# Loading each group's weights in three parts, behind three row tiles in a row, in a fused gated-mix forward and backward kernel

## The chip, the cores and the metric

One Trainium2 chip, one core. The time is the device time of the whole program in microseconds (us). The kernel before takes 1472.38 us (median of 3 runs, 1470.64 to 1474.87). All runs told here fell in the fast state; verdicts are faster, same or slower at 2%, with a 95% interval.

## The reference, cut to what matters

```python
def _fwd_reference(A_x, A_w_r, A_w_i, B_x, B_w_gate, B_w_up, B_w_down, gate_w):
    x = A_x                                                  # 1 x 2048 x 576, bf16
    g = _sigmoid((x * gate_w).sum(-1, keepdims=True))
    a = irfft2(rfft2(x) * (A_w_r + 1j * A_w_i))              # spectral branch
    b = (gelu(x @ B_w_gate) * (x @ B_w_up)) @ B_w_down       # F = 4608
    return g * a + (1 - g) * b
# reference: the output and the gradients of all seven differentiable inputs for one grad_out
```

## The kernel before

The hidden dimension F = 4608 is worked through in 18 groups g of 256 columns (`FG`). Each group has four row tiles m of 512 rows. In a row tile TensorE forms `z` (gradient of the hidden value, from wdT) and `xy` (gate and up, from wgu); ACT and DVE make `A`, `dHg`, `dHu` of them, which go to HBM scratch. Between these matmuls TensorE does the weight gradients of the group before and steps of the spectral branch, whose PSUM tile `pf` is taken from the pool of `z`, which has one buffer.

The loads and stores of the groups in this argument are issued by one engine, SP (`LD = nc.sync`), in program order.

```python
unit = Unit(ctx.enter_context(tc.tile_pool(name="unit", bufs=NUNIT, side="right")))   # NUNIT = 19
wpool = hstack.enter_context(tc.tile_pool(name="wpool", bufs=2, side="right"))
pz = ps1.enter_context(tc.tile_pool(name="pz", bufs=1, space=PSUM))     # z, and pf from group 1 on
# ... cut ...
def load_w(g):                       # nine DMAs
    fsl = slice(g * FG, (g + 1) * FG)
    wgu = wpool.tile([P, 5, 2 * FG], BF16, tag="wgu", name="wgu")
    wdT = wpool.tile([P, 5, FG], BF16, tag="wdT", name="wdT")
    for k, w in enumerate((B_w_gate, B_w_up)):
        cols = slice(k * FG, (k + 1) * FG)
        LD.dma_start(wgu[:, 0:4, cols], w[0:512, fsl].rearrange("(c p) f -> p c f", p=P))
        for r in (LO, HI):
            LD.dma_start(wgu[r, 4, cols], w[512:D, fsl])
    LD.dma_start_transpose(wdT[:, 4:5, :], B_w_down[fsl, DCH[4][0]:D])
    LD.dma_start_transpose(wdT[:, 0:4, :], B_w_down[fsl, 0:512])
    LD.dma_start(wdT[LO, 4, :], wdT[HI, 4, :])
    return wgu, wdT
# ... cut: one step of the inverse transform, inside s1 ...
    vps = pftile()                   # PSUM from pz
    # four matmuls into vps
    Vt = unit([2, DF], name="Vt")    # a buffer of the shared ring
    nc.scalar.copy(Vt[:], vps[:, :, :DF])
    LD.dma_start(dst[i], Vt[:])      # scr_p <- Vt
# ... cut: end of a row tile (g, m), pr = 4 g + m ...
    flush(len(stores) - 1)           # issues the waiting stores (A, dHg, dHu; o) but the last entry
    if pr == 1:
        early_loads()                # wts[1] = load_w(1), and gwb, a row of gate_w
    # ... cut ...
    if m == 0 and g >= 1 and g + 1 < NG:
        wts[g + 1] = load_w(g + 1)
```

Behind the groups a last stage of jobs reads the scratch back by transposing DMAs (`pin`), multiplies with w_down, w_gate and w_up transposed (`wd_all`, `wgT`, `wuT`) and writes two outputs.

```python
for i, (kind, t) in enumerate(jobs):
    if i > 1 and wT_loads:           # six loads: in front of jobs 2 to 7
        load_wuT(*wT_loads.pop(0))
    # ... cut ...
    else:                            # the last job
        gate_grad()                  # 80 matmuls of one column, then two stores of single numbers (out_7)
        x_last(t)
```

## Time and profile before

| | before |
|---|---|
| span of the profiled run | 1469.9 us |
| TensorE busy | 1446.1 us, 98% |
| DVE, ACT busy | 58%, 47% |
| half clock ahead of the end | 3.41 us from 285.58 us, and again from 1446.11 us |

The busy shares, the waits of TensorE, the timelines around the one wait of a row tile and the clock behind it stand in the prediction.

### The profile page before, as it was taken

Reading aid. Unit: us, or ns where it says so; the run is one execution under the profiler, and the core shown is the slowest. Engines: PE = TensorE matmul, PEld = TensorE weight load, DVE = VectorE, ACT = ScalarE, POOL = GpSimd, SP = SyncE. Lnnn points to the kernel's source line nnn. Section 1 sums busy time; section 2 is a strip of 40 time slices with the busy share of each in tenths; the row PEclk is TensorE's granted clock in tenths of the full one; section 3 lists DMA queues with packets and bytes.
Section 4 is the critical chain, followed back from the end, with each engine's and each line's share of the span. In section 5 each row is a group of like instructions: output and inputs, shape, how many; then the busy total and the mean of one; then the engine's idle time right before and its main releaser. Section 6 shows DMA issues by size and latency. Waiting matters only on the chain.

```text
span 1469.9 us, 30099 instructions
## 1 busy us (share of the span) xinstructions
PE 1446.1 (98%) x11808; PEld 1069.9 (73%) x11808; DVE 846.4 (58%) x2258; ACT 691.4 (47%) x1355; POOL 118.7 (8%) x203
## 2 busy tenths in 40 slices
PE   7999999899999999999999999999999999999998
PEld 5766667577677777677677677678877777777776
DVE  7697677788888887676776776774000541211110
ACT  5776666566766676666666666663000000000000
POOL 1000011010011001001001001000000110000000
PEclk9999999999999999999999999999999999999999
DMA  5144444444544434443534544757999997878773
GB/s 189 55 132 122 126 120 120 137 132 128 154 141 145 122 101 139 124 119 114 145 106 116 151 123 109 166 132 152 268 187 201 216 199 161 172 156 164 158 150 75
DMA packets 483963, 210.49 MB, mean 143 GB/s; under 512 B 307883, under 2 KB 473932, under 8 KB 483820
## 3 DMA queue, kind: packets, MB, share of 16 engines
q1 hardware_dynamic: 474220, 188.06, 54.1%
q0 software_dynamic: 7792, 19.49, 4.4%
q8 instruction: 92, 1.51, 0.5%
q10 hardware_dynamic: 1808, 1.02, 0.2%
q14 instruction: 51, 0.42, 0.1%
HBM read 40.89 MB, written 93.82 MB: 92 GB/s over the span
## 4 chain that ended last, share of the span: by engine, by line
PE 91%; DVE 4%; DMA 1%; ACT 1%; issue 0%; SPq 0%; DVEq 0%; ACTq 0%
PE acc L930 28%; PE wps L440 17%; PE xy L330 16%; PE wps L423 9%; PE z L318 8%; PE wps L453 2%; PE xy L325 2%; PE pf L683 2%; PE z L321 1%; PE pf L671 1%; PE pf L490 1%; DMA pin<-scr 1%; PE fx L490 0%; DVE Vt L510 0%; DVE om L383 0%
## 5 line engine op out<-in xcount | busy, mean ns | idle before, releaser
L930 PEld LDWEIGHTS <-pin 128*128 128x128 bf16 x3456 | 338.6, 98 | 89.4 <-DMA pin<-scr 3.4
L330 PE MATMUL xy<-wgu,xT 128*128 128x512 bf16 x1152 | 271.5, 380 | 0.0
L440 PEld LDWEIGHTS <-xn 128*128 128x128 bf16 x2304 | 225.3, 98 | 32.4 <-issue 0.2
L330 PEld LDWEIGHTS <-xT 128*128 128x128 bf16 x1152 | 106.9, 98 | 137.3 <-issue 30.4
L343 ACT ACTIVATE da<-z,omg 128x256 bf16<-128x256 f32 x288 | 113.4, 475 | 149.6 <-PE z L321 146.5
L947 ACT COPY bo<-acc 128x288 f32<-128x288 f32 x32 | 12.8, 399 | 311.2 <-PE acc L930 286.6
L423 PE MATMUL wps<-dB,A 128*128 128x288 bf16 x1152 | 154.2, 286 | 0.0
L318 PE MATMUL z<-wdT,dOT 128*128 128x256 bf16 x1152 | 139.2, 275 | 6.6 <-ACT Vt L634 5.1
L930 PE MATMUL acc<-wd_all,pin 128*128 128x288 bf16 x1152 | 142.9, 286 | 2.8 <-DMA pin<-scr 2.8
L930 PE MATMUL acc<-wgT,pin 128*128 128x288 bf16 x1152 | 145.3, 288 | 0.0
L930 PE MATMUL acc<-wuT,pin 128*128 128x288 bf16 x1152 | 143.6, 286 | 0.0
L423 PEld LDWEIGHTS <-A 128*128 128x128 bf16 x1152 | 112.7, 98 | 35.6
L440 PE MATMUL wps<-dHg,xn 128*128 128x256 bf16 x1152 | 134.4, 273 | 0.0
L440 PE MATMUL wps<-dHu,xn 128*128 128x256 bf16 x1152 | 131.5, 273 | 0.0
L318 PEld LDWEIGHTS <-dOT 128*128 128x128 bf16 x1152 | 111.9, 98 | 24.7 <-issue 10.9
L349 ACT ACTIVATE q<-xy 128x512 bf16<-128x512 f32 x144 | 86.0, 597 | 69.3 <-PE xy L330 65.7
L1004 DVE SCALAR_TENSOR_TENSOR f32t<-gwf,dlog,b16t 128x576 f32<-128x576 f32 x16 | 13.1, 818 | 182.7 <-DMA b16t<-dxa_scr 182.7
L356 DVE TENSOR_SCALAR s<-q 128x512 bf16<-128x512 bf16 x144 | 42.8, 297 | 100.6 <-ACT q L349 98.9
L373 ACT ACTIVATE om<-s 128x512 bf16<-128x512 bf16 x144 | 92.0, 639 | 8.3 <-DVE s L357 8.1
L374 ACT ACTIVATE s<-s 128x512 bf16<-128x512 bf16 x144 | 90.9, 631 | 4.6
L446 POOL DMA_DIRECT2D out_dram<-dw x67 | 48.8, 729 | 539.9 <-ACT dw L401 277.4
L357 DVE TENSOR_TENSOR s<-xb,s 128x512 bf16<-128x512 bf16 x144 | 61.3, 426 | 49.7 <-ACT xb L354 43.6
(182 smaller groups left out, 1807.2 us busy)
## 6 DMA issues: line engine op xcount, KB each, us to landing
scr<-A SPq DMA_DIRECT2D x144, 128.0 KB, 2.1
scr<-dHg SPq DMA_DIRECT2D x144, 128.0 KB, 2.0
scr<-dHu SPq DMA_DIRECT2D x144, 128.0 KB, 2.0
out_dram<-dw POOLq DMA_DIRECT2D x67, 128.0 KB, 2.6
wd_all<-in_B_w_down_dram SPq DMA_DIRECT2D x3, 1728.0 KB, 13.2
out_dram<-dwd POOLq DMA_DIRECT2D x34, 144.0 KB, 2.4
scr_p<-Vt SPq DMA_DIRECT2D x32, 144.5 KB, 2.2
Vp<-scr_p SPq DMA_DIRECT2D x16, 289.0 KB, 3.2
```

The costliest lines, as they stand in the source:

```text
L318: nc.tensor.matmul(zo(t), lhsT=dOT[:, ci, t, :], rhs=wdT[:, ci, :], start=(t % 4 < 2 and ci == 0), stop=False)
L330: nc.tensor.matmul(xy[k][:, t % 2, :], lhsT=xT[:, ci, t, :], rhs=wgu[:, ci, :], start=False, stop=(ci == 3))
L343: nc.scalar.activation(da[:, tt, :], z[:, tt, k, :], ACT.Copy, scale=omg32[:, t:t + 1])
L349: nc.scalar.activation(q[:], xy[:, :, 0:FG], ACT.Square)
L356: V.tensor_scalar(s[:], q[:], A_GELU, 1.0, op0=ALU.mult, op1=ALU.add)
L357: V.tensor_tensor(s[:], xb[:], s[:], op=ALU.mult)
L373: nc.scalar.activation(om[:], s[:], ACT.Sigmoid, scale=-2.0 * C_GELU)
L374: nc.scalar.activation(s[:], s[:], ACT.Sigmoid, scale=2.0 * C_GELU)
L423: nc.tensor.matmul(wps[:, :288], lhsT=tl(0, t)[:, fch * P:(fch + 1) * P], rhs=dB[:, t, h * 288:(h + 1) * 288], start=(t == 0), stop=(t == ...
L440: nc.tensor.matmul(wps[:, cc, :], lhsT=xn[:, t, (c0 + cc) * P:(c0 + cc + 1) * P], rhs=tl(k, t), start=(t == 0), stop=(t == T - 1))
L446: wst[0].dma_start(ov[:, c0:c0 + TPB, fsl], dw[:])
L930: nc.tensor.matmul(acc[:, :288], lhsT=src[:, r, :], rhs=w_of(r)[:, h * 288:(h + 1) * 288], start=(first and r == 0), stop=(last and r == F ...
```

## The change

The intent is to spread the loads: w_gate's part of the next group behind row tile 0, w_up's behind row tile 1, w_down's transposes behind row tile 2. The row of gate_w moves behind row tile 3 of group 0.

```diff
-    def load_w(g):
+    wts = {}
+
+    def load_w(g, part):
+
         fsl = slice(g * FG, (g + 1) * FG)
# ... cut: the two tiles are made in part 0 ...
+        if part < 2:
+            w, cols = (B_w_gate, B_w_up)[part], slice(part * FG, (part + 1) * FG)
             LD.dma_start(wgu[:, 0:4, cols], w[0:512, fsl].rearrange("(c p) f -> p c f", p=P))
             for r in (LO, HI):
                 LD.dma_start(wgu[r, 4, cols], w[512:D, fsl])
+        else:
+            LD.dma_start_transpose(wdT[:, 4:5, :], B_w_down[fsl, DCH[4][0]:D])
+            LD.dma_start_transpose(wdT[:, 0:4, :], B_w_down[fsl, 0:512])
+            LD.dma_start(wdT[LO, 4, :], wdT[HI, 4, :])
# ... cut: the unused load_dOT goes; the first group is loaded in three calls ...
             flush(len(stores) - 1)
-            if pr == 1:
-                early_loads()
+            if m < 3 and g + 1 < NG:
+                load_w(g + 1, m)
+            if pr == 3:
+                LD.dma_start(gwb[:], gate_w.partition_broadcast(P))
# ... cut ...
-            if m == 0 and g >= 1 and g + 1 < NG:
-                wts[g + 1] = load_w(g + 1)
```

The instructions of TensorE, ACT, DVE and GpSimd keep their order and number; only what they wait for differs. SP has the same 985 DMAs in another order.

## The prediction

> **What bounds the kernel now.** I read the busy shares first, then the waits of TensorE, then the place of the largest wait on three engines, then the granted clock around it.
>
> The first line of the page settles how much any change of loads can win:
>
> ```profile
> PE 1446.1 (98%) x11808; PEld 1069.9 (73%) x11808; DVE 846.4 (58%) x2258; ACT 691.4 (47%) x1355; POOL 118.7 (8%) x203
> PE 91%; DVE 4%; DMA 1%; ACT 1%; issue 0%; SPq 0%; DVEq 0%; ACTq 0%
> ```
>
> TensorE is busy 1446.1 of 1469.9 us, and the chain that ended last (second line) is 91% TensorE. Work on TensorE is the same in both kernels, instruction for instruction, so at most the 23.8 us of idle time, plus whatever slows it while it is busy, can change. Where the idle time lies, the list of TensorE's waits says (what waited, for what: total us, times, longest):
>
> ```profile
> PE z L318 <- ACT Vt L634: 5.1, 1, 5.1
> PE tp L283 <- DMA xn<-in_A_x_dram: 4.8, 1, 4.8
> PE acc L930 <- DMA pin<-scr: 2.8, 2, 1.5
> PE fx L490 <- DVE xT L292: 2.3, 1, 2.3
> PE z L318 <- ACT Y L496: 1.2, 2, 0.8
> ```
>
> No wait for a weight tile (wgu, wdT) is in it: the weights arrive in time, and spreading them cannot win anything by bringing them earlier. The start (xn), the head (fx) and the last stage (pin) do not touch these loads. What is left is one wait of 5.1 us, once in 18 groups. The timelines of the three engines there (start, us, what, idle before and its releaser), PE first, then ACT, then the load and store queue SP:
>
> ```profile
> 278.33 1.91 PE L440 MATMUL wps<-dHg,xn 128*128 128x256 bf16 x16
> 285.39 3.43 PE L318 MATMUL z<-wdT,dOT 128*128 128x256 bf16 x16 [5.15 <-ACT Vt L634]
> ...
> 278.89 0.38 ACT L401 CAST dwd<-wps 128x288 bf16<-128x288 f32 x1
> 284.70 0.64 ACT L634 CAST Vt<-pf 128x578 bf16<-128x578 f32 x1 [5.43 <-DMA scr_p<-Vt]
> ...
> 272.73 0.37 SPq L389 DMA_DIRECT2D scr<-dHu  x1
> 273.15 0.46 SPq L217 DMA_DIRECT2D wgu<-in_B_w_gate_dram  x1
> 273.66 1.20 SPq L219 DMA_DIRECT2D wgu<-in_B_w_gate_dram  x2
> 274.90 0.59 SPq L217 DMA_DIRECT2D wgu<-in_B_w_up_dram  x1
> 275.53 1.15 SPq L219 DMA_DIRECT2D wgu<-in_B_w_up_dram  x2
> 276.73 1.26 SPq L220 DMA_TRANSPOSE wdT<-in_B_w_down_dram  x1
> 278.03 1.29 SPq L221 DMA_TRANSPOSE wdT<-in_B_w_down_dram  x1
> 279.42 0.54 SPq L222 DMA_DIRECT2D wdT<-wdT  x1
> 280.05 0.54 SPq L609 DMA_DIRECT2D out_dram<-o  x1
> 280.69 0.44 SPq L610 DMA_DIRECT2D out_dram<-o  x1
> 281.22 4.47 SPq L635 DMA_DIRECT2D scr_p<-Vt  x3
> ```
>
> Read it from the end. TensorE wants the accumulator z at 280.24, but z shares a single buffer with the spectral tile pf, which ACT empties into a Vt tile (L634) only at 284.70, because that Vt tile still waits for an older Vt to be stored. That older Vt was written by ACT at 272.99 to 273.63; its store is issued at 281.22 and lands at 284.62 (3.40 us later in the chain of waits). The store was ready 7.6 us before it was issued: nine weight DMAs held the queue from 273.15 to 279.96, 6.8 us.
>
> One thing more, from the view by windows around the wait (stretch, length, busy time of the engines, then PEclk, DMA share, GB/s):
>
> ```profile
> 285.40:289.00 3.60, 3.60 (x20) 2.35 (x21) 1.06 (x2) 0.00 (x0) 0.71 (x1) 0.53 0.68 201
> ```
>
> The granted clock is 0.53, where every stretch around it has 1.00. That is why the 16 matmuls of z take 3.43 us here and 1.91 us in other row tiles: the wait is paid again in busy time.
>
> **What the Trainium skill says.** The page "TensorE: Matmul & The Clock Gate", in "What's actually happening", says that an idle window of some 3.4 us drops the TensorE clock to 4/8 and that a busy window of the same length restores it. The trace agrees: 5.15 us idle, then 0.53 of the clock over 3.6 us; its clock record is half speed for 3.41 us. The page "DMA: Bandwidth & Descriptors", in "Anatomy of one DMA", says that a wait for a semaphore happens on the issuing sequencer ahead of dispatch[...]. The trace agrees[...]: SP issues strictly one after the other, so whatever stands behind a waiting or long DMA is late, and the Vt stores land 2.2 us (median) after issue. The same page, in "Rules for kernel authors", advises to issue a DMA early and wait on it late; the third part of the new load is issued later than now, so this is where the change could lose.
>
> **The change part by part.** Nothing is removed or added in number: the queue has the same DMAs with the same bytes, in another order. Before, the nine DMAs of a group's weights stand together behind the first row tile m=0 (for the first group behind m=1, with gate_w's row). After, three (w_gate) stand behind m=0, three (w_up) behind m=1, and two transposes with one copy behind m=2; gate_w's row comes after m=3.
>
> Hold of the queue at one point, from the rows above: part 1 is 0.46+1.20, about 1.75 us with gaps; part 2 is 0.59+1.15, about 1.8; part 3 is 1.26+1.29+0.54 plus the copy's wait, about 3.3 to 4. So the longest hold falls from 6.8 to about 4 us.
>
> Around 273 us: part 1 ends at about 274.9. The two stores of o were ready then (DVE finished o at 273.76), and are out by about 275.6. The Vt store is issued at about 275.6 to 276 and not 281.22, and lands 3.4 us later at 279.0 to 279.4. ACT gets to its next Vt at 279.27 at the earliest (behind L401). It runs to about 280.0, and TensorE wants z at 280.24. The 5.15 us go, with perhaps 0.2 left. With the idle stretch goes the half clock: 3.41 us at half speed is 1.7 us of work. Sum: 5.15 + 1.7 = 6.85 us.
>
> **What could be given back.** I laid the new order over the old trace: each store ready when its producer ended, each DMA as long as it was, each landing as late as it was. The weights then come in time: for groups 2 to 17 the last of wdT lands 6 to 15 us ahead of the first z (a row tile takes 12 to 15 us, and the third part lags the start of its row tile by 0 to 6 us). The narrow one is group 1: in group 0 DVE lags, the third part is issued at 89.4 to 92 us, and z of group 1 starts at 95.4. With the usual 3.3 us from issue to landing (median of the wdT DMAs) it lands at 94; with the longest seen, 5.7 us, at 96.4, a loss of 1 us. I put 0.3 us. Stores behind part 2 and 3 get up to 4 us later than now; the one that a Vt then waits for is o at 309 us (landing 310.2 before, 313.7 after, while ACT wants the tile at 311.6), and TensorE needs it by 314.5, so it just fits. I put 0.3 us on such things.
>
> Total: 1472.4 - 6.85 + 0.6 = 1466.1, rounded to 1466 us, a ratio of 0.9957.
>
> **The rivals.**
> 1. *Nothing changes* (1470 to 1473). The wait would have another cause than the queue, or would move to the next full tile. Against it: the releaser named is the landing of scr_p, and its store stands right behind the weights. For it: ring slots and the eight DMA semaphores, each waited on before it is used again, could hold the Vt elsewhere.
> 2. *A new wait takes its place.* The transposes, now last, come late at each group: 17 groups times 1 us would be 1483 us or more. Against it: margins of 6 us and more, but for group 1. Or a later hold of 4 us meets another Vt store: one event would give back 2 to 7 us (1468 to 1473), as a wait over some 3.4 us costs the clock too.
> 3. *Contention eases* since 640 KB no longer come at one point. Against a gain: no wait for these transfers is on TensorE's list, and its matmuls (L330 median 379 ns, longest 390) are not stretched in the windows of the loads. Worth 0.
>
> **Range and chances.** The idle time tied to these loads is one event, so the gain is capped near 7 us, half a per cent. Runs of before spread from 1470.6 to 1474.9, which is as wide as a third of the range. I take 1462.5 to 1471. Faster by over 2% would need 29 us, more than all of TensorE's idle time: 0.01. Slower by over 2% needs a stall of 1.7 us in each group: 0.01. Within 2%: 0.98.
>
> **What would show it.** Right: TensorE's list of waits has no "z <- ACT Vt" of 5 us, its idle time is about 18.5 us, not 23.8, its busy time falls by about 1.7 us though it runs the same instructions, the mean granted clock goes from 0.998 to nearly 1, and SP issues the scr_p store within 3 us of the Vt. Wrong: a line where z or xy waits for DMA wdT or wgu; a stretch with the clock near 0.5 elsewhere; a wait of ACT for out_dram<-o or scr_p over 3 us near the end of a row tile; or the old wait still there with another releaser.

## More of the kernel before

In the last stage TensorE waits twice for a `pin` tile (timeline of TensorE: start, us, what, idle time before it and its releaser):

```profile
1106.83 8.99 PE L930 MATMUL acc<-wd_all,pin 128*128 128x288 bf16 x72 [1.36 <-DMA pin<-scr]
1117.27 4.95 PE L930 MATMUL acc<-wd_all,pin 128*128 128x288 bf16 x39 [1.45 <-DMA pin<-scr]
```

And in the last microseconds (the list of DMA issues: what, engine, count, KB, us from issue to landing) the store of the gate's gradient, 512 single numbers, takes long for 1 KB:

```profile
out_dram<-dgw POOLq DMA_DIRECT2D x1, 1.0 KB, 15.3
```

## The result, and the profile after

The changed kernel takes 1464.15 us (median of 4 runs, 1463.28 to 1466.38); before took 1471.51 us beside it (median of 4, 1469.18 to 1474.87). The ratio is 0.9951, interval 0.9927 to 0.9974: within 2%, and clear of 1.

TensorE's waits in the changed kernel (lines of the program have moved by three: L318 is L321, L634 is L637; in the last stage by one):

```profile
PE xy L333 <- issue: 7.6, 48, 0.2
...
PE acc L929 <- DMA pin<-scr: 1.6, 1, 1.6
PE z L321 <- ACT Y L499: 1.2, 2, 0.8
```

The wait of z for Vt is gone, and none for a weight tile has come. The new first line is no wait: 48 gaps of 0.16 us. The page tells where they come from, in its line of busy times:

```profile
PE 1433.0 (98%) x11723; PEld 1068.6 (73%) x11808; DVE 846.0 (58%) x2258; ACT 690.7 (47%) x1355; POOL 118.3 (8%) x203
```

There are 11723 matmuls where before had 11808, but as many weight loads (PEld, 11808): 85 records of matmuls are missing, so the busy time is too low and the idle time too high. Compare weight loads, not busy times, when the counts differ.

Around the old wait, TensorE, then ACT, then SP:

```profile
278.47 1.91 PE L443 MATMUL wps<-dHg,xn 128*128 128x256 bf16 x16
280.22 1.91 PE L321 MATMUL z<-wdT,dOT 128*128 128x256 bf16 x16
...
279.02 0.38 ACT L404 CAST dwd<-wps 128x288 bf16<-128x288 f32 x1
279.30 0.64 ACT L637 CAST Vt<-pf 128x578 bf16<-128x578 f32 x1
...
273.27 0.46 SPq L223 DMA_DIRECT2D wgu<-in_B_w_gate_dram  x1
273.78 1.20 SPq L225 DMA_DIRECT2D wgu<-in_B_w_gate_dram  x2
275.07 0.53 SPq L612 DMA_DIRECT2D out_dram<-o  x1
275.70 0.41 SPq L613 DMA_DIRECT2D out_dram<-o  x1
276.21 4.08 SPq L638 DMA_DIRECT2D scr_p<-Vt  x3
```

The Vt store is issued at 276.21, 2.4 us after ACT wrote the tile, and the trace has it landed at 279.20. ACT goes from its dwd straight to the next Vt, and z starts with no idle time and takes 1.91 us for its 16 matmuls, not 3.43. The view by windows has the clock whole:

```profile
280.20:283.80 3.60, 3.44 (x30) 2.29 (x30) 3.46 (x9) 1.30 (x4) 0.07 (x1) 1.00 0.74 218
```

To see where each microsecond went, I lined up the starts of the 11808 weight loads of both traces, which come in the same order:

| weight load | before | changed | difference, us |
|---|---|---|---|
| last one ahead of the old wait | 279.98 | 280.11 | +0.14 |
| first of z in that row tile | 285.40 | 280.22 | -5.18 |
| first of xy's main part there | 289.08 | 282.29 | -6.79 |
| last stage, ahead of any wait for pin | 1105.06 | 1098.25 | -6.80 |
| behind the waits for pin | 1188.21 | 1180.06 | -8.15 |
| behind the gate's gradient | 1450.64 | 1440.82 | -9.82 |
| end of the span | 1469.93 | 1462.42 | -7.51 |

So 5.3 us of idle time and 1.6 us of half clock went in group 4, and from there to the last stage, 800 us later, the offset stays within 0.02 us: between these two profiles no other group gained or lost anything. The last stage, which the change does not touch, then moved by -1.35 (waits for pin), -1.67 (a half clock behind the gradient's small matmuls, in the trace of before only) and +2.31 (the end). The last is seen in the DMA issues of the last 7 us (the last store of out_1) and of the whole run (the gate's gradient):

```profile
out_dram<-b16t SPq DMA_DIRECT2D x1, 72.0 KB, 5.1
out_dram<-dgw POOLq DMA_DIRECT2D x1, 1.0 KB, 15.9
```

In before the same last store took 2.7 us. Its issue is 9.8 us earlier now, but it lands about 1.5 us behind the gradient's slow store in both kernels (1468.65 against 1467.21; 1461.13 against 1459.62), and that one started only 8.1 us earlier.

### The profile page after: what moved, and what is told of

Its sections match the earlier page's. It is cut to its first block, busy times and chain, and to the rows that moved or that the text cites. A ratio compares the mean times of both kernels' runs of the same rounds, so it can differ in the third digit from the quotient of the medians.

```text
span 1462.4 us, 30015 instructions
## 1 busy us (share of the span) xinstructions
PE 1433.0 (98%) x11723; PEld 1068.6 (73%) x11808; DVE 846.0 (58%) x2258; ACT 690.7 (47%) x1355; POOL 118.3 (8%) x203
## 4 chain that ended last, share of the span: by engine, by line
PE 92%; DVE 3%; issue 1%; ACT 1%; DMA 0%; DVEq 0%; ACTq 0%
PE acc L929 29%; PE wps L443 17%; PE xy L333 16%; PE wps L426 9%; PE z L321 8%; PE wps L456 2%; PE xy L328 2%; PE pf L686 2%; PE z L324 1%; PE pf L674 1%; PE pf L493 1%; PE fx L493 0%; DVE Vt L513 0%; DMA pin<-scr 0%; PE pf L632 0%
## 5 line engine op out<-in xcount | busy, mean ns | idle before, releaser
L333 PE MATMUL xy<-wgu,xT 128*128 128x512 bf16 x1067 | 257.7, 380 | 9.6 <-issue 7.6
L333 PEld LDWEIGHTS <-xT 128*128 128x128 bf16 x1152 | 106.8, 98 | 137.3 <-issue 29.9
L321 PE MATMUL z<-wdT,dOT 128*128 128x256 bf16 x1152 | 137.7, 273 | 1.5 <-ACT Y L499 1.2
L321 PEld LDWEIGHTS <-dOT 128*128 128x128 bf16 x1152 | 111.2, 98 | 18.8 <-issue 5.6
```

The costliest lines, as they stand in the source:

```text
L321: nc.tensor.matmul(zo(t), lhsT=dOT[:, ci, t, :], rhs=wdT[:, ci, :], start=(t % 4 < 2 and ci == 0), stop=False)
L333: nc.tensor.matmul(xy[k][:, t % 2, :], lhsT=xT[:, ci, t, :], rhs=wgu[:, ci, :], start=False, stop=(ci == 3))
```

## The experiments

Theory: in one group of 18 the nine weight DMAs stood in SP's queue ahead of a Vt store, so ACT got a Vt buffer late, so the single pf/z buffer came free late, so TensorE idled 5.15 us and then ran at half clock. Rivals: spreading eases contention a little in every group; or the split as such, or the first group's loads, bring it. The first four runs shared runs of before (1475.55 us on that chip), the next four another set (1471.99 us), the last two a third (1471.04 us). All results were correct.

### 1. The split in group 4 alone

Before's placement in all groups but one.

```diff
-            if m < 3 and g + 1 < NG:
-                load_w(g + 1, m)
+            if g + 1 < NG:
+                for part in (([m] if m < 3 else []) if g == 4
+                             else range(3) if m == (1 if g == 0 else 0) else ()):
+                    load_w(g + 1, part)
```

> The kernel before, with the weights of the next group split in three parts in group 4 alone (the group whose row tile 2 waited 5.15 us); all other groups load at one point, as before. Theory (the hold of the queue in group 4 is the whole of it): the whole gain, 5.15 us of idle time and 1.7 us of half clock, so 1464 to 1466 us, ratio about 0.995; no wait of z for Vt of more than 0.3 us and no stretch at half clock before the last 30 us. Rival (spreading eases contention in every group, 0.4 us each in 17): 1/17 of the gain, 1471 us. Rival (the first group's earlier load or gate_w's later row): no gain, 1471 us.

Measured: 1467.56 us, ratio 0.9944 (0.9929 to 0.9959). The weight loads are 5.58 us ahead of before at z, and 7.20 us ahead once the place of the old half clock is past. One wait of z for Vt is left, 0.41 us where at most 0.3 was expected; it is not at the old place but at 307.88, at the first z of group 5, where that Vt waits for the landing of a store of o that stood behind the third part. The time in us is above the expected range only because before is 4 us slower on this chip; the ratio is as expected. One group brings the whole gain, so neither contention in every group nor parts elsewhere are needed. The run does keep gate_w's later row, so it tells nothing on that; the next one does.

### 2. The split everywhere but in group 4

```diff
-            if m < 3 and g + 1 < NG:
-                load_w(g + 1, m)
+            if g + 1 < NG:
+                for part in ((range(3) if m == 0 else ()) if g == 4 else [m] if m < 3 else []):
+                    load_w(g + 1, part)
```

> The changed kernel with group 4 alone loading at one point again. Theory: the wait and the half clock are back in row tile 2 of group 4, 5.2 us idle (4.8 to 5.6) and 3.4 us at half speed, so 1471 us, ratio about 1.000. Rival (contention in every group): 16/17 of the gain stays, 1465 us.

Measured: 1477.57 us, ratio 1.0011 (0.9996 to 1.0026): the gain is gone, with 16 groups and the first one still in parts and gate_w's row still late. The wait is back, 6.1 us where 5.2 was expected (the store took 4.35 us to land and not 3.40), in the list of waits, and the clock in the windows of the wait and behind it:

```profile
PE z L321 <- ACT Vt L637: 6.1, 1, 6.1
```

```profile
280.40:286.50 6.10, 0.10 (x1) 0.00 (x0) 5.93 (x15) 0.62 (x1) 0.00 (x0) 0.70 0.56 149
286.50:290.00 3.50, 3.43 (x18) 2.34 (x19) 0.21 (x1) 0.02 (x1) 0.71 (x1) 0.55 0.66 197
```

The half clock lasts 6.83 us in the clock record, from 282.82, but 3.75 us of it fall into the wait itself and cost nothing; the rest, some 3.1 us with TensorE at work, costs about 1.5 us.

### 3. Two parts, then one, in group 4

```diff
-            if m < 3 and g + 1 < NG:
-                load_w(g + 1, m)
+            if g + 1 < NG:
+                for part in ({0: (0, 1), 1: (2,)}.get(m, ()) if g == 4 else [m] if m < 3 else []):
+                    load_w(g + 1, part)
```

> The changed kernel, but in group 4 the first two parts together behind row tile 0 and the third behind row tile 1. The hold in front of the Vt store is 3.6 us and not 1.75 or 6.8. From the trace of before: store issued at 277.4, landed at 280.8, so z waits about 1.3 us (0.8 to 1.8). Theory of the two costs: an idle stretch of 1.3 us, too short to drop the clock, so that no half clock appears and the loss is 1.3 us, not 3: 1465.5 us. Rival (any wait there costs the clock in proportion, a quarter of 1.7 us): a stretch at half clock of about 0.8 us is seen in the clock record. Rival (contention): same as the changed kernel.

Measured: 1470.34 us, ratio 0.9963 (0.9944 to 0.9982). The wait and the window behind it:

```profile
PE z L321 <- ACT Vt L637: 1.9, 1, 1.9
```

```profile
282.40:286.00 3.60, 3.59 (x29) 2.28 (x29) 3.46 (x10) 1.32 (x4) 0.00 (x0) 1.00 0.57 160
```

The wait is 1.94 us, just over the range given (the store was issued at 278.13, not 277.4), and the clock stays whole. So the wait grows with the hold of the queue (1.75 us of hold: none; 3.6: 1.94; 6.8: 5.15 and 6.1), and the clock is a second cost that only the long ones paid.

How long is long? The Trainium skill ("TensorE: Matmul & The Clock Gate", "What's actually happening") says of the drop that it takes an idle window of about 3.4 us and that the windows run free. The traces agree with the second: in each of them the changes of the clock lie whole multiples of 3.413 us apart (in before, 285.58 and 1446.11 are 340 of them apart). They do not agree with the first. In this run's last stage a wait of 2.04 us was followed by 3.41 us at half speed, from 1112.16, while in run 1 one of 2.62 us was not (run 3's line, then run 1's):

```profile
1111.70 8.46 PE L930 MATMUL acc<-wd_all,pin 128*128 128x288 bf16 x54 [2.04 <-DMA pin<-scr]
...
1112.28 7.89 PE L930 MATMUL acc<-wd_all,pin 128*128 128x288 bf16 x63 [2.62 <-DMA pin<-scr]
```

Run 3's wait lies in one window; run 1's is cut by the end of a window at 1111.15 into 1.49 and 1.13 us. With all 12 traces cut into such windows, every window at full clock with 2.03 us or more of idle time (30 of them) was followed by half clock, and none with up to 1.95 us was. (Five more drops stand behind the gate gradient's small matmuls; see the last section.) So the wait of 1.94 us could not cost the clock, and that of 5.15 us had to, since at least 2.57 us of it fall into one window wherever the windows lie (an estimate from these figures).

### 4. The loads at one point, but a ring of its own for Vt

```diff
-NUNIT = 19
+NUNIT = 18
+    vtp = hstack.enter_context(tc.tile_pool(name="vtp", bufs=3, side="right"))
-                Vt = unit([2, DF], name="Vt")
+                Vt = vtp.tile([P, 2, DF], BF16, tag="vt1", name="Vt")
```

> The kernel before with its loads at one point in all groups, but the Vt tile of the inverse transform's first step (L634) in a ring of three buffers of its own, one unit buffer fewer in the shared ring (18 for 19, for space). The queue is held 6.8 us as before and the Vt store still issues about 8 us after its Vt is written, but the next Vt does not need that buffer. Theory (queue hold, then buffer, then accumulator): the gain is there though no load moved, 1464 to 1467 us, and SP's timeline at the weights is unchanged. Rival (moving or spreading the loads itself brings it): 1471 us. Risk: a shared ring with one buffer fewer makes a new wait elsewhere (a wait of ACT or DVE for a DMA of o or Vp), up to 5 us.

A plain twentieth buffer in the shared ring did not fit into SBUF and was never run. Measured: 1469.09 us, ratio 0.9954 (0.9938 to 0.9970). SP, then ACT:

```profile
278.98 0.54 SPq L223 DMA_DIRECT2D wdT<-wdT  x1
...
280.78 1.44 SPq L636 DMA_DIRECT2D scr_p<-Vt  x3
...
278.12 0.64 ACT L635 CAST Vt<-pf 128x578 bf16<-128x578 f32 x1
```

The queue is held as long as before and the Vt store is as late (280.78), yet ACT writes the next Vt at 278.12 and z starts at 279.67, in time. No load moved, and the gain is there: at xy the weight loads are 7.34 us ahead of before. What the hold costs depends on the buffer behind it. (ACT was also some 1.3 us earlier at the first Vt here, since the ring has other neighbours; and two half clocks in the last stage, 1.7 us each, are in this profile.)

### 5. All three parts at one point, one row tile later

```diff
-            if m < 3 and g + 1 < NG:
-                load_w(g + 1, m)
+            if g + 1 < NG:
+                for part in (range(3) if m == 1 else ()):
+                    load_w(g + 1, part)
```

> All three parts of a group's weights at one point, as before, but behind row tile 1 of every group and not behind row tile 0 (group 0 has them there in both). The queue is held 6.8 us at one point in each group. Theory (where the hold meets a Vt store is what matters, not the number of parts): the wait of group 4 is gone; of 32 Vt stores laid over the trace of before, one (at 561 us, landing at 565.4 where the next Vt wants its buffer at 562.7) makes a wait of z of about 1.3 us (0 to 2), too short for the clock. Ratio 0.995 to 0.997, about 5.5 us less than before. Rival (the split into parts brings the gain): ratio 1.000. Rival (later loads are late for the next group): waits of z or xy for wgu or wdT; by the trace of before the last transpose lands 14 to 20 us ahead of z, so none.

Measured: 1464.48 us, ratio 0.9944 (0.9932 to 0.9956). The wait is gone, and the 1.3 us that I expected at 561 us did not come: TensorE's list has no wait of z for Vt. Splitting is not needed; the nine DMAs only must not stand ahead of those stores.

### 6. The third part behind row tile 3

```diff
-            if m < 3 and g + 1 < NG:
-                load_w(g + 1, m)
+            if g + 1 < NG:
+                for part in {0: (0,), 1: (1,), 3: (2,)}.get(m, ()):
+                    load_w(g + 1, part)
```

> The changed kernel with its third part (the two transposes and the copy) behind row tile 3 and not behind row tile 2, that is with about 13 us less lead. From the trace of before, the transposed weights would land 2 to 11 us after z of the next group wants them, 4.9 us in the mean over 17 groups. Theory (a late load is the cost that the change could have had): a wait of z for wdT in each of the 17 groups of 3 to 6 us, with the half clock behind most of them (1.7 us each[...]): 70 to 115 us more than the changed kernel, 1535 to 1580 us. Rival (DVE and ACT catch up during the wait, so that the queue's lag shrinks and the waits are short): 20 to 50 us more.

Measured: 1573.14 us, ratio 1.0688 (1.0671 to 1.0706), slower. The waits, and one of them on TensorE's timeline:

```profile
PE z L321 <- DMA wdT<-in_B_w_down_dram: 79.7, 17, 9.5
```

```profile
333.29 3.60 PE L321 MATMUL z<-wdT,dOT 128*128 128x256 bf16 x16 [4.93 <-DMA wdT<-in_B_w_down_dram]
```

All 17 groups wait, 4.7 us in the mean (4.9 expected). The span is 106.8 us above the changed kernel's; 79.7 are the waits, and the clock record has 14 stretches at half speed between 98 and 1061 us, 82 us in all. TensorE was at work in 58 us of them, which at half speed costs about 29 us and so goes with the other 27. This is the price that the change would have paid with one row tile less of lead.

### 7. The gate's gradient three row tiles earlier

```diff
         for i, (kind, t) in enumerate(jobs):
+            if (kind, t) == ("g", 13):
+                gate_grad()
# ... cut ...
-                gate_grad()
                 x_last(t)
```

> The changed kernel with the gate's gradient (80 matmuls with one column, the copy, and the store of 576 single numbers) three row tiles earlier and not just before the last one. In the traces of before and of the changed kernel that store takes 14.5 to 15.3 us to land, and the last store of out_1 lands 1.4 to 1.5 us after it in both, though its issue is 9.8 us earlier in the changed kernel: 2.75 and 5.05 us from issue to landing. Theory (the end is set by the scattered store, so the changed kernel gives back 2.3 us there): the last store lands 2 to 3 us after issue, 2 to 3 us less than the changed kernel, ratio to before about 0.993. Rival (the last store is slow for another reason): 5 us again and no gain. Risk: half clock behind the 80 small matmuls, 1.7 us, as in some runs now.

Measured: 1470.15 us, ratio 0.9982 (0.9964 to 1.0000), and unusually wide, 1464.56 to 1473.25; the profile is of a slow one, 1473.19. The tail did what the theory says, the last store landing 1.6 us after issue. But in this execution 8 us were lost in the middle; the waits there, and the windows over the time in which the gradient's store was under way (1411 to 1433 us):

```profile
PE acc L929 <- DMA pin<-scr: 8.1, 1, 8.1
```

```profile
1411.00:1422.00 11.00, 11.00 (x93) 8.78 (x91) 0.00 (x0) 0.00 (x0) 1.47 (x3) 1.00 0.73 70
1422.00:1434.00 12.00, 3.93 (x32) 2.90 (x30) 0.00 (x0) 0.00 (x0) 0.00 (x0) 0.86 1.14 38
```

The last columns are the clock, the busy share of the DMA engines and GB/s: 0.73 and 1.14 busy, at 70 and 38 GB/s where the changed kernel moves 152 and 144 in the same windows. While the store of 576 single numbers, issued by GpSimd, is under way, the transposes that SP issues come through at less than half of that rate. The Trainium skill ("DMA: Bandwidth & Descriptors", "Issuing engines are not separate DMA queues") says that all issuers share the same 16 DMA engines and interleave; this run agrees, and the interleaving cost 8.1 us here. The expectation was wrong in its sum.

### 8. The wuT loads with gaps

```diff
-            if i > 1 and wT_loads:
+            if i in (2, 3, 5, 6, 8, 9) and wT_loads:
```

> The changed kernel with the six loads of the transposed up weights in the last stage in front of jobs 2, 3, 5, 6, 8, 9 and not of six jobs in a row (2 to 7). In the traces so far a job with such a load takes the queue 10.3 to 10.8 us, one without 5.4 to 6.2 us, and TensorE 8.9 us; after the sixth in a row TensorE waits 1.6 to 4.3 us for a pin tile, and in some runs the clock is halved for 3.4 us behind it. Theory (the same fault one stage later: loads at one stretch of the queue use up the lead of the others): no wait of acc for pin over 0.3 us, and no half clock before the end stretch: 2 to 4 us less than the changed kernel, ratio to before about 0.992 to 0.993. Rival (the last stage is bound by the transfers over all of it): the waits come later, no gain.

Measured: 1462.11 us, ratio 0.9932 (0.9919 to 0.9945). TensorE goes through the six jobs without a wait (one merged line where there were three):

```profile
1054.58 70.60 PE L929 MATMUL acc<-wd_all,pin 128*128 128x288 bf16 x575
```

The half clock came up all the same, behind the gradient's 80 small matmuls, so that half of the expectation failed. The interval also overlaps that of the changed kernel (0.9927 to 0.9974, on another chip), so a gain over it is likely but not shown by the times.

### 9 and 10. The gate's gradient as one row

On run 8's kernel: dlog as the weights and x as the moving columns, so that the result is a row and its store one piece of 1152 bytes. Run 9 has it at run 7's early place, run 10 at the old one.

```diff
-            gps = pacc.tile([P, 512], F32, tag="acc", name="gps")
-            # 80 matmuls: out 128 x 1, then two stores, one number per partition
+            gps = acc_pair()
+            for h in range(2):
+                for t in range(T):
+                    nc.tensor.matmul(gps[h][0:1, :288], lhsT=dlog_bf[:, t:t + 1],
+                                     rhs=xn[:, t, h * 288:(h + 1) * 288], start=(t == 0), stop=(t == T - 1))
+            # two copies to a [1, 576] tile, one store
```

> The kernel of the run with spread wuT loads, with the gate's gradient at the early place of the slow run, but formed as one row (32 matmuls with dlog as the weights and x as the moving 288 columns) and stored as one row of 1152 contiguous bytes in place of 576 single numbers. Theory (the scattered store held the DMA engines, 0.7 to 1.1 busy at 38 to 70 GB/s, and so the pin transposes for 8 us): the row lands in 2 to 4 us, no wait of acc for pin over 0.5 us after 1380 us, the last store of out_1 lands 1.6 to 2.8 us after issue; TensorE pays 1.6 us more for the 32 wider matmuls (some 3.9 us for 2.3) and no half clock. Ratio to before 0.992 to 0.993. Rival (the early place itself is bad: the small matmuls or the order of the queue): the pin wait of about 8 us stays and the ratio is 0.997 or more.

> The same row form at the old place, just before the last row tile, with the spread wuT loads. Theory (the end is set by the scattered store): the last store of out_1 lands 1.6 to 2.8 us after issue, not 2.8 to 5.05, and no half clock behind the gradient's matmuls, against 1.6 us more on TensorE: 0 to 2 us less than the run with spread wuT loads alone, ratio to before 0.991 to 0.993. Rival (the last store is slow for another reason): its landing stays at 3 us or more and the ratio is 0.994 for the wider matmuls.

Measured: 1460.85 us, ratio 0.9926 (0.9912 to 0.9939), and 1460.55 us, ratio 0.9925 (0.9911 to 0.9938). Neither profile has a wait of acc for pin or a half clock before the end. In run 10 (DMA issues):

```profile
out_dram<-dgw POOLq DMA_DIRECT2D x1, 1.1 KB, 1.6
```

15.9 us have become 1.6, and the last store of out_1 lands in 1.6 us too, in both runs. The early place is harmless with the row store, so in run 7 the scattered store did the harm and not the place. (Run 9 differs from run 7 in the wuT loads and the form of the matmuls too; but the changed kernel, with run 7's wuT loads, has no wait in that stretch, and what run 7's TensorE waited for is a transfer.) These are the fastest versions measured; the differences among runs 8, 9 and 10 are within their intervals.

## Why the prediction was right

The prediction was 1466 us; 1464.15 was measured, a gain of 7.4 us by the medians where 6.4 was predicted. The interval of the ratio means 4 to 11 us, so the times alone do not tell these two apart; the profiles do. The range was said to be three times as wide as the spread of before; by its own figures (4.3 us in 8.5) it is twice.

*TensorE sets the time, no weight is late, so one wait is all there is.* Right: runs 1 and 2 put the whole gain into group 4, and the offset of the weight loads does not move for 800 us after it.

*Store held, Vt late, pf held, z late.* Right link by link. Predicted: store at 275.6 to 276, landing 279.0 to 279.4, ACT at 279.27; measured 276.21, 279.20, 279.30. (The two stores of o hold the queue 1.17 us by the lines that the prediction shows, so its own sum should have been 276.1; the landing made it up, 2.99 us and not 3.40.) Run 3 shortens the hold and the wait shrinks, run 4 cuts the link from the store to the buffer, run 5 moves the hold; each takes the wait away or down. That the link from pf to z runs through the one PSUM buffer was not tried by itself; it rests on the pool's one buffer and the waits of the profile.

*5.15 us of idle time and 1.7 of half clock.* Measured 5.3 and 1.6, together 6.93 for 6.85. Run 3, with a wait and no half clock, shows that these are two costs.

*0.6 us given back* (late transposes in group 1, late stores). In the changed kernel's profile this was 0, by a narrow margin. In group 1 the last of wdT landed at 94.20 (94 predicted), 1.3 us ahead of z, which waits 0.83 us for ACT, as before; in the other groups the lead was 3.6 to 10.2 us, where 6 to 15 was predicted. The late store of o was foreseen at the right place: the first z of group 5 started without a wait in the changed kernel, but waited 0.41 us in run 1 and 0.67 us in run 7, for the Vt that waits for o. So the 0 is in part luck. The transposes' risk was real in kind, as run 6 shows.

*A wait over some 3.4 us costs the clock too.* It did here, but the limit is lower: 2.03 us of idle time in one window was enough (run 3).

*What the prediction did not have* is the last stage: 0.7 us net between these two profiles (-1.35, -1.67 and +2.31). Waits for pin and the half clock behind the gradient come and go from run to run with either placement of the loads, so I do not count them to the change, and that part of the gain measured is luck; the end at the scattered store is a limit that swallows what comes earlier.

*What would show it.* One sign failed as stated: idle time on the page rose from 23.8 to 29.4 us and did not fall to 18.5, for want of 85 records. The mean clock rose only to 0.999, as the last 2.3 us of this profile, behind TensorE's last matmul, are at half clock.

## What to carry to other kernels

On a queue that one engine issues in order, a block of loads costs nothing by itself; it costs where a store behind it frees a buffer that the busiest engine needs, so look for the releaser of the wait, then for what stood in the queue between "ready" and "issued". Move, split or give a buffer, whichever is cheapest: each alone brought the same half per cent here, while 13 us less lead for one part cost 7%. When a kernel is 98% busy, read off the ceiling of the gain first, and count the lost clock behind a wait along with the wait: in these traces it was lost from about 2 us of idle time on, depending on where the clock's windows fell.

## What the Trainium skill lacked or had wrong

- "TensorE: Matmul & The Clock Gate" says that the clock drops after an idle window of about 3.4 us. In these traces less was enough: 2.03 us or more of idle time within one window of 3.413 us dropped it in all 30 cases, up to 1.95 us in none. A drop can also begin inside the wait and cost less than its length: the 6.83 us at half speed in run 2 cost about 1.5 us.
- The same page speaks of idle TensorE. In 5 of the 10 profiles with the gate gradient's 80 one-column matmuls (before, runs 3, 4, 6 and 8), which the profile counts as 2.34 us of busy time, 3.41 us of half clock followed them; in the 2 profiles with 32 matmuls of 288 columns in their place, none did. In these five at least 2.22 of the 2.34 us lay in one window of the clock, in the other five at most 2.14, which fits such matmuls being counted as idle (not tried by itself).
- "DMA: Bandwidth & Descriptors" explains why small descriptors are slow, but has no figure for a store of single 2-byte numbers: the two stores that carry 576 of them (512 and 64) took 14.4 to 21.5 us each to land, one row of the same 1152 bytes 1.6 to 1.9 us, and while the scattered ones were under way a DMA transpose from another issuer came 8.1 us late for TensorE.
